# Two-tile residual transfers, a GpSimd-written mask period and an even queue split in an attention and gMLP kernel

## The chip, the cores and the metric

The kernel runs on one NeuronCore of one Trainium2 chip. The metric is device time in microseconds (us) of one execution. Before the change it is 1194.28 us, the median of six executions, which lie between 1193.59 and 1197.21 us. The engines are called by the profile's names: PE (TensorE matmul), PEld (its weight loads), DVE (VectorE), ACT (ScalarE), POOL (GpSimd) and SP (SyncE). Each engine works through its own instructions in order. SP does no arithmetic; it issues DMA transfers. POOL and ACT can issue them too. An issue occupies the issuing engine's queue for some time, and the data lands later.

## The reference

The input is `x` of 2048 tokens by 576 features in bf16. Four layers follow each other, A, B, A, B, each added to `x` after a layer norm. Both A layers share their weights, and so do both B layers.

```python
# A: 32 heads of 18 features; a token sees itself and 7 earlier tokens, 2 apart
idx = pos[:, None] - (arange(8) * 2)[None, :];  mask = idx >= 0
logits = einsum('bhsd,bhswd->bhsw', q, kg) * 18 ** -0.5     # kg, vg: k, v gathered at idx
o = einsum('bhsw,bhswd->bhsd', softmax(where(mask, logits, -1e9)), vg);  return o @ wo
# B: gated MLP that mixes the tokens
z = gelu(x @ w_in);  z1 = z[..., :2304];  z2 = layernorm(z[..., 2304:])
return (z1 * (einsum('ts,bsf->btf', w_sp, z2) + b_sp)) @ w_out

x = x + A(layernorm(x));  x = x + B(layernorm(x))           # twice
```

## The kernel before

Between layers the residual stream lies in DRAM, in the input for the first layer and in `xres[li]` (f32) after it. What the next layer multiplies is held on chip: `xnT` is the normalised `x` with features on partitions and tokens along the free axis. It is filled in tiles of 128 tokens, for most tiles by a DMA transpose on SP (`ln_T`, L249).

**Layer A** (`layer_A`, L322) has two parts. Its instructions are issued in the order in which the code is written.

*Preparation.* `VW` (L373) makes the values of one attention tile. `PG` (L384) multiplies one 128-feature block `d` of queries or keys (`qk`) for one block of 512 tokens (`cc`) and leaves it in a staging tile `stg`, or, for `d` of 3 and 4 in the first token half of the first layer, in the space of the later weight tile `win2a`. When a staging tile is full, its pieces of heads are moved by DMA to `QK`, where a head has a group of 32 partitions to itself; these are the *head moves* (L421). A half of the tokens (`cc` 0 and 1, or 2 and 3) takes 40 of them. They are dealt out in turn to the queues given by name: with `(nc.gpsimd, nc.sync)` each gets every second one, and with `q2 = (nc.gpsimd, nc.sync, nc.gpsimd)` SP gets every third.

Rows 18 to 31 of each 32-partition group hold a bit pattern that makes the dot product of query and key itself put the window's mask in (`build_window_rows`, L115). The first 16 partitions' rows are written to DRAM as `win_period` (L174), loaded into `pat` (`load_pat`, L176) and copied into `QK` by DVE (`fill_window_rows`, L188).

In the first layer (`li == 0`) there is a prologue ahead: `x` is loaded, `S_` takes bn_stats on DVE, `E_` adds epsilon on DVE, `R_` raises to the power -1/2 on POOL, and `A_` normalises on DVE. Tiles 0 to 3 go through PE transposes and an ACT copy into `xnT` (`T_pe`, L561), all others through DMA transposes on SP (`T_`, L569). Those of tiles 12 to 15 stand on SP behind all head moves of the first token half (L631).

*The loop* (L698). Attention works on 19 tiles `t` of 112 queries with 16 earlier keys, each in two halves of the heads, which makes 38 steps `s = 2t + half`. A step runs the scores of the next step (`L_mm`, L426), the exponential on ACT (`EXP`, L440), the values product (`PV`, L447) and then whatever the table has for this step. After every odd step `PV` sends the tile's output through a DMA transpose on SP into `oT` (L467), a ring of 7 tiles of 128 tokens.

The table spreads the rest over the steps (L661 to L683). The remaining `PG` of the second token half stand at steps 0 to 12; the first of them, block 0 of `cc` 3, reads `xnT` of tiles 12 to 15. For output tile `i` of 128 tokens, whose last attention tile is `t`, the step is `s = 2t + 6` in the first layer for `t < 8`, then `2t + 5`, and less at the end:

```python
at(s - 5, XO, i)        # load the residual rows, SP
at(s, WO, i, 0); at(s + 1, WO, i, 1)     # PE: times wo; DVE adds the residual rows into x_new
at(s + 1, LN_STATS, i); at(s + 2, LN_XN, i)
at(s + 2, XST, i)       # store x_new, SP
if i < NS - 1: at(s + 4, LN_T, i)        # transpose for the next layer, SP
```

`XO`'s tile has three buffers and `x_new` four, each of one output tile. So SP carries, for every output tile, a load, a store and two transposes, and in steps 0 to 12 half of the head moves as well.

The program gives the transfers of SP and ACT eight completion counters in turn, and POOL's another eight; a transfer that takes a counter again waits until the transfer that had it last has landed.

**Layer B** (`layer_B`, L714) is three long runs of matmuls: `z` (L782), the token mixing with the gate (`z1` L860 and `gate` L878), and the output (L932), which loads the residual rows and stores the new ones one tile a transfer. The change leaves it alone.

Of the kernel before, what the change touches and what calls it, by code (L numbers as in the profile page):

```python
# [10 lines left out]
ALU = mybir.AluOpType  # L11
AX = mybir.AxisListType
f32 = mybir.dt.float32
bf16 = mybir.dt.bfloat16
# [4 lines left out]
P = 128  # L19
D = 576  # L20
# [7 lines left out]
EPS = 1e-5  # L28
MR = 32 - DH
# [33 lines left out]
class K:  # L63
# [48 lines left out]
        self.xn_rr = 0  # L112
        self.deferred = []

    def build_window_rows(self, c):  # L115

        nc = self.nc
        R = c.tile([P, 2, MR, 16], bf16, name="win_rows")
        self.pat = self.consts.tile([P, 2, 272], bf16, name="win_pat")
        self.patpad = self.consts.tile([P, PADL], bf16, name="win_patpad")
        n = c.tile([P, 3], i32, name="win_n")
        g = c.tile([P, 3], i32, name="win_g")
        bits = c.tile([P, 5, 3], i32, name="win_bits")
        vf = c.tile([P, 5, 3], f32, name="win_vf")
        uu = c.tile([P, 4, 2], f32, name="win_uu")  # L130
        half = WB / 2
        nc.gpsimd.iota(n[:], pattern=[[1, 3]], base=15, channel_multiplier=1)
        nc.gpsimd.memset(R[:, 0, 0:8, :], half)
        nc.gpsimd.affine_select(out=R[:, 0, 0:8, :], in_=R[:, 0, 0:8, :], compare_op=ALU.is_ge, fill=-half,
                                base=1, pattern=[[2, 8], [-1, 16]], channel_multiplier=0)
# [24 lines left out]
        def pads():  # L160
            nc.gpsimd.memset(self.pat[:], 0.0)
            nc.gpsimd.memset(self.patpad[:], 0.0)
            for j in range(4):
                nc.gpsimd.affine_select(out=self.patpad[:], in_=self.patpad[:], compare_op=ALU.not_equal, fill=1.0,
                                        base=-32 * j - 31, pattern=[[0, PADL]], channel_multiplier=1)

        def part1(eng):
            nc.vector.tensor_scalar(out=vf[:], in0=bits[:], scalar1=-2.0, scalar2=1.0, op0=ALU.mult, op1=ALU.add)
            nc.vector.tensor_scalar_mul(out=R[:, :, 0:8, :], in0=R[:, :, 0:8, :], scalar1=vf[:, 4, 1:2])
            nc.vector.tensor_tensor(out=uu[:], in0=vf[:, 0:4, 0:2], in1=vf[:, 0:4, 1:3], op=ALU.add)  # L170
            nc.vector.tensor_scalar_mul(out=R[:, 0, 8:12, :], in0=vf[:, 0:4, 1:2].to_broadcast([P, 4, 16]), scalar1=half)
            nc.vector.tensor_scalar_mul(out=R[:, 1, 8:12, 0:2], in0=uu[:, :, 0:1].to_broadcast([P, 4, 2]), scalar1=0.5)
            nc.vector.tensor_scalar_mul(out=R[:, 1, 8:12, 2:16], in0=uu[:, :, 1:2].to_broadcast([P, 4, 14]), scalar1=0.5)
            self.dma(one[:].rearrange("a r (p f) -> p (a r) f", f=16), R[0:16].rearrange("p a r f -> p (a r) f"), eng=eng)  # L174

        def load(eng):  # L176
            for j in range(4):
                self.dma(self.pat[32 * j + DH:32 * j + 32, :, 0:256], one[:].rearrange("a r x -> r a x"), eng=eng)
        self.load_pat = load
        return part0, pads, part1  # L180
# [141 lines left out]
    def layer_A(self, li):  # L322
        nc, tc, cfg = self.nc, self.tc, self.cfg
        S, NT, XW, NS = cfg.S, cfg.NT, cfg.XW, cfg.NS
# [15 lines left out]
        oT = main.tile([P, 5, RING * P], bf16, name="oT")  # L340
        sb_cm = tc.tile_pool(name=f"A{li}_sb", bufs=2, reuse_waits="tile")
        sb = sb_cm.__enter__()
        if self.right is None:
            self.open_right()
        R = self.right
# [129 lines left out]

        tails = {}

        def XO(i):
            tails[i] = dict(xo=sb.tile([P, D], x_prev_dt, name="xo", tag="xo", bufs=3))
            self.dma(tails[i]["xo"][:], x_prev[i * P:(i + 1) * P, :], eng=nc.sync)  # L480

        def WO(i, hh):
            st = tails[i]
            if hh == 0:
                st["x"] = sb.tile([P, D], f32, name="x_new", tag="x_new", bufs=4)
            r0 = (i % RING) * P
            pw = self.PT_tile([P, 512], f32, "pw")
            for c in range(5):
                nc.tensor.matmul(pw[:, 0:288], lhsT=oT[:, c, r0:r0 + P], rhs=wo_sb[:, c, hh * 288:(hh + 1) * 288],  # L489
                                 start=(c == 0), stop=(c == 4))  # L490
            hs = slice(hh * 288, (hh + 1) * 288)
            nc.vector.tensor_tensor(out=st["x"][:, hs], in0=pw[:, 0:288], in1=st["xo"][:, hs], op=ALU.add)

        def XST(i):
            self.dma(self.xres[li][i * P:(i + 1) * P, :], tails[i]["x"][:])

        def LN_STATS(i):
            tails[i]["ln"] = self.ln_stats(sb, tails[i]["x"], P, want_nmr=False)
# [11 lines left out]
        if li == 0:  # L510
# [19 lines left out]
            warm = self.PT_tile([P, 512], f32, "warm")  # L530
            for _ in range(46):
                nc.tensor.matmul(warm[:, 0:P], lhsT=self.ident[:], rhs=self.ident[:], start=True, stop=True)
            rows = self.build_window_rows(sb)
            nc.scalar.copy(out=v_ext[:, :, :, DH:DH + 1], in_=self.ones[:, None, None, :].to_broadcast([P, NT, H, 1]))
            rows[0]()
            mvs = sb.tile([P, NS, 2], f32, name="lnx_mv", tag="lnx_mv", bufs=1)
# [6 lines left out]
                        nc.vector.bn_stats(out=st[:, s, :], in_=xts[i][:, s * 288:(s + 1) * 288])  # L543
                    nc.vector.bn_aggr(out=mvs[:, i, :], in_=st[:])

            def E_(i0, n):
                nc.vector.tensor_scalar_add(out=rstds[:, i0:i0 + n], in0=mvs[:, i0:i0 + n, 1], scalar1=EPS)

            def R_(i0, n):
                nc.gpsimd.tensor_tensor(out=rstds[:, i0:i0 + n], in0=rstds[:, i0:i0 + n],  # L550
                                        in1=self.neg_half[:, 0:1].to_broadcast([P, n]), op=ALU.pow)
            xns = {}

            def A_(*tiles):
# [15 lines left out]
                for i in tiles:  # L570
                    self.ln_T(xns.pop(i), i * P, P)
            S_(0)
            E_(0, 1)
            R_(0, 1)
            S_(1)
            E_(1, 1)
            R_(1, 1)
            A_(0)
            T_pe(0)
            VW(0, 0, False)  # L580
            VW(0, 1, False)
            S_(2)
            A_(1)
            T_pe(1)
            VW(1, 0, False)
            S_(3)
            E_(2, 2)
            R_(2, 2)
            rows[1]()
            setup_bufs(nc.gpsimd)  # L590
            rows[2](nc.scalar)
            A_(2, 3)
            T_pe(2)
            T_pe(3)
            VW(1, 1, False)
            x_load(sb.tile([P, 4, D], bf16, name="x_in3", tag="x_in", bufs=2)[:], 12, 4, nc.sync)
            S_(4, 5)
            E_(4, 2)
            R_(4, 2)
            VW(2, 0, False)  # L600
            VW(2, 1, False)
# [1 line left out]
            A_(4, 5)  # L603
            T_(4, 5)
            S_(7)
            E_(6, 2)
            R_(6, 2)
            S_(8)
            A_(6, 7)
            T_(6, 7)  # L610
            self.load_pat(nc.sync)
            S_(9, 10, 11)
            E_(8, 4)
            R_(8, 4)
            S_(12)
            A_(8, 9, 10, 11)
            T_(8, 9, 10, 11)
            self.fill_window_rows(QK, 0)
            S_(13, 14, 15)
            E_(12, 4)  # L620
            order = [(d, 0) for d in range(4)] + [(d, 1) for d in range(4)] + [(4, 0), (4, 1)]
            for k_, (d, cc) in enumerate(order):
                for qk in ((1, 0) if d < 4 else (0,)):
                    PG(d, qk, cc, False, (nc.gpsimd, nc.sync) if d in (0, 4) else q2)
                if k_ == 3:
                    VW(3, 0, False)
                    VW(3, 1, False)
                if k_ == 5:
                    R_(12, 4)
                    A_(12, 13, 14, 15)  # L630
# [42 lines left out]
                at(2 * t - 2 + hh, VW, t, hh, 2 * t - 2 + hh >= PG_END and hh == 0)  # L673
        for i in range(NS):
            t = -(-(i + 1) * P // QT) - 1
            s = 2 * t + (6 if li == 0 and t < 8 else 5 if t < NT - 5 else 4 if t < NT - 3 else 3)
            at(s - 5, XO, i)
            at(s, WO, i, 0)
            at(s + 1, WO, i, 1)
# [364 lines left out]
```

The softmax here doesn't subtract the row's maximum and nothing guards it: scores larger than these inputs give would overflow.

## Time and profile before

| | |
|---|---|
| median of six executions | 1194.28 us |
| the profiled execution's own time | 1194.59 us |
| its span from first to last instruction | 1192.8 us |
| PE busy | 1179.4 us (99%) |
| DVE / ACT / POOL busy | 545.5 / 378.5 / 276.9 us |
| mean granted clock of PE | 0.999 |
| first layer, up to the first matmul of B | 0 to 136 us |
| its loop, from the first `PV` on | 48.6 to 136 us |
| first B layer | 136 to 602 us |
| third layer (A) | 602 to 723 us |
| last layer (B) | 723 to 1193 us |
| xo transfers on SP in the A and B layers | 16 of 144 KB, 48 of 288 KB |
| xres stores on SP | 48 of 288 KB |

The profile is of one execution. Its span is 1.8 us shorter than that execution's own time. PE hardly ever rests, so what moves the time is either work added to or taken from PE, a stretch in which PE has to wait, or a stretch in which the clock granted to PE is below 1. [...]

In the timeline, a row is: start in us, length in us, engine, line, operation, output<-input, number of instructions, and in brackets the idle time before it and what ended it. A `q` behind an engine's name (SPq) marks its queue's own work, such as issuing a transfer.

### The profile page before, as it was taken

The numbers are of one execution on the slowest core, as the hardware profiler recorded it, in microseconds if no ns is written. First come the engines' busy times: TensorE is split into PE (matmuls) and PEld (weight loads), VectorE is DVE, ScalarE is ACT, GpSimd is POOL, SyncE is SP. The second block draws the span as 40 slices with busy tenths as digits, with TensorE's granted clock in tenths as the row PEclk, the third lists the DMA queues.
The fourth block names the chain that finished last, engine by engine and source line by source line (L and its number), as shares of the span: only waits on it lengthen the run. The fifth ranks groups of instructions, "written<-read, shape, count | busy, mean of one in ns | idle before, by whom it ended". The sixth has DMA issues, their size and how long they took to land.

```text
span 1192.8 us, 20790 instructions
## 1 busy us (share of the span) xinstructions
PE 1179.4 (99%) x8554; PEld 619.8 (52%) x8554; DVE 545.5 (46%) x1202; ACT 378.5 (32%) x597; POOL 276.9 (23%) x382
## 2 busy tenths in 40 slices
PE   8999999999999999999999999999999999999998
PEld 5566544444444444457755775444444444444676
DVE  9677676333233233245556776763233233232321
ACT  5578677210110110202156786760110110111000
POOL 4668774000000000001153877530000000000000
PEclk9999999999999999999999999999999999999999
DMA  8789791000000000049656799900000000001332
GB/s 197 152 192 230 173 241 38 23 3 10 12 12 12 12 2 10 15 140 286 168 102 119 175 242 190 215 13 10 12 12 1 12 12 12 12 1 33 119 105 73
DMA packets 178791, 101.21 MB, mean 85 GB/s; under 512 B 135039, under 2 KB 160047, under 8 KB 178696
## 3 DMA queue, kind: packets, MB, share of 16 engines
q1 hardware_dynamic: 165400, 78.14, 29.5%
q0 software_dynamic: 6480, 15.99, 5.2%
q10 hardware_dynamic: 6816, 5.77, 1.6%
q8 instruction: 67, 1.10, 0.4%
q14 instruction: 28, 0.23, 0.1%
HBM read 42.39 MB, written 16.53 MB: 49 GB/s over the span
## 4 chain that ended last, share of the span: by engine, by line
PE 94%; DMA 1%; ACT 0%; issue 0%; DVE 0%; SPq 0%; DVEq 0%; ACTq 0%
PE pg L878 42%; PE pz L860 12%; PE po L932 12%; PE pz L782 11%; PE pp L400 4%; PE pw L489 3%; PE O_ps L455 3%; PE pv L377 3%; PE L_ps L435 2%; PE pzs L782 1%; DMA oT<-o_t 1%; ACT P_sb L444 0%; DMA QK<-win2a 0%; PE pt L473 0%; SPq L77 0%
## 5 line engine op out<-in xcount | busy, mean ns | idle before, releaser
L878 PE MATMUL pg<-Wq,Z 128*128 128x512 bf16 x2304 | 502.8, 379 | 0.0
L878 PEld LDWEIGHTS <-Z 128*128 128x128 bf16 x2304 | 225.3, 98 | 272.0
L882 DVE TENSOR_TENSOR g_tmp<-pg,ln_xn 128x512 f32<-128x512 f32 x144 | 99.6, 692 | 428.0 <-PE pg L878 428.0
L872 ACT ACTIVATE z1T<-pz 128x1024 bf16<-128x1024 f32 x72 | 73.7, 1024 | 513.8 <-PE pz L860 513.6
L77 POOL DMA_DIRECT2D wout<-in_B_w_out_dram x4 | 4.2, 1062 | 604.6 <-PE pg L878 604.6
L932 PE MATMUL po<-wout,Z 128*128 128x288 bf16 x1152 | 141.4, 286 | 0.0
L444 ACT ACTIVATE P_sb<-L_ps 128x896 bf16<-128x896 f32 (+1 forms) x152 | 126.7, 887 | 41.8 <-PE L_ps L435 41.1
L860 PE MATMUL pz<-xnT,w 128*128 128x512 bf16 (+1 forms) x640 | 136.0, 380 | 0.0
L932 PEld LDWEIGHTS <-Z 128*128 128x128 bf16 x1152 | 112.7, 98 | 28.8
L782 PEld LDWEIGHTS <-xnT 128*128 128x128 bf16 (+1 forms) x800 | 66.3, 97 | 80.9 <-issue 23.7
L782 PE MATMUL pz<-win2a,xnT 128*128 128x512 bf16 x384 | 104.8, 380 | 0.0
L883 DVE TENSOR_TENSOR Z<-g_tmp,z1T 128x512 bf16<-128x512 f32 x144 | 99.7, 692 | 10.8 <-DVE g_tmp L882 1.4
L860 PEld LDWEIGHTS <-w 128*128 128x128 bf16 (+1 forms) x640 | 51.0, 97 | 80.1 <-issue 27.1
L400 PE MATMUL pp<-xnT,wqk_sb 128*128 128x512 bf16 x360 | 83.5, 382 | 0.0
L796 ACT ACTIVATE zp<-pz 128x1024 bf16<-128x1024 f32 x64 | 65.5, 1024 | 36.7 <-PE pz L782 34.1
L242 POOL TENSOR_SCALAR ln_xn<-x_new,ln_mv,ln_rstd 128x576 bf16<-128x576 f32 x32 | 73.4, 2294 | 2.7
L942 DVE TENSOR_TENSOR x_new<-po,xo 128x288 f32<-128x288 f32 (+1 forms) x64 | 28.8, 456 | 87.9 <-PE po L932 83.9
L782 PE MATMUL pz<-win2b,xnT 128*128 128x512 bf16 (+1 forms) x256 | 65.8, 380 | 0.0
L798 DVE CUSTOM_DVE_ANT_0 Z<-zp 128x1536 bf16<-128x1536 bf16 x32 | 56.4, 1761 | 15.6 <-ACT zp L796 15.5
L77 POOL DMA_DIRECT2D QK<-stg x81 | 50.2, 624 | 38.6 <-DVE stg L369 13.9
L377 PE MATMUL pv<-wv_sb,xnT 128*128 128x288 bf16 (+1 forms) x380 | 56.2, 285 | 2.4 <-ACT xnT L567 2.4
L400 PEld LDWEIGHTS <-wqk_sb 128*128 128x128 bf16 x360 | 33.3, 98 | 36.5 <-issue 0.8
(111 smaller groups left out, 889.9 us busy)
## 6 DMA issues: line engine op xcount, KB each, us to landing
xres<-x_new SPq DMA_DIRECT2D x48, 288.0 KB
xo<-xres SPq DMA_DIRECT2D x48, 288.0 KB
wout<-in_B_w_out_dram POOLq DMA_DIRECT2D x4, 1296.0 KB, 8.0
w<-in_B_w_in_dram SPq DMA_DIRECT2D x16, 256.0 KB
QK<-stg POOLq DMA_DIRECT2D x53, 72.0 KB, 3.8
QK<-stg SPq DMA_DIRECT2D x41, 72.0 KB
xo<-in_A_x_dram SPq DMA_DIRECT2D x16, 144.0 KB
win2a<-in_B_w_in_dram POOLq DMA_DIRECT2D x6, 288.0 KB, 4.7
```

The lines of the kernel that those rows point to most:

```text
L242: e.tensor_scalar(out=xn[:nrows, 0:D], in0=x_t[:nrows, :], scalar1=mv[:nrows, 0:1], scalar2=rstd[:nrows, 0:1], op0=ALU.subtract, op1=ALU.mult)
L377: nc.tensor.matmul(pv[:nk, 0:288], lhsT=self.xnT[:, c, QT * t:QT * t + nk], rhs=wv_sb[:, c, hh * 288:(hh + 1) * 288], start=(c == 0), stop ...
L400: nc.tensor.matmul(pp[:, :], lhsT=w, rhs=self.xnT[:, c, PADL + cc * 512:PADL + (cc + 1) * 512], start=(c == 0), stop=(c == 4))
L444: nc.scalar.activation(out=P_bufs[(2 * s + jp) % 4][:nk, :, :, 0:nq], in_=Lv[:nk, :, :, 0:nq], func=ACT.Exp, scale=scale)
L782: nc.tensor.matmul(pzvs[ci][:, sub * 512:sub * 512 + w], lhsT=self.xnT[r0:r1, c, PADL + i * P:PADL + (i + 1) * P], rhs=win2(c)[r0:r1, c0 + ...
L796: nc.scalar.activation(out=zp[:, c0:c0 + cn], in_=pzvs[ci][:, 0:cn], func=ACT.Gelu_apprx_tanh, accum_out=sums[:, ci:ci + 1])
L860: nc.tensor.matmul(pz1s[q // 2][:, q % 2, :], lhsT=w1[r0:r1, c, sub * P:(sub + 1) * P], rhs=self.xnT[r0:r1, c, PADL + q * 512:PADL + (q + ...
L872: nc.scalar.activation(out=z1T[:, q2 * 512:(q2 + 2) * 512], in_=pz1s[q2 // 2][:, :, :].rearrange("p a b -> p (a b)"), func=ACT.Gelu_apprx_ ...
L878: nc.tensor.matmul(pg[:, :], lhsT=Z[:, jj, i, sub * P:(sub + 1) * P], rhs=Wq[q][:, i, :], start=(i == 0), stop=(i == NS - 1))
L882: nc.vector.tensor_tensor(out=tmp[:], in0=pg[:, :], in1=bsp[:, qs], op=ALU.add)
L883: nc.vector.tensor_tensor(out=uT(jj)[:, sub, qs], in0=tmp[:], in1=z1Ts[jj, sub][:, qs], op=ALU.mult)
L932: nc.tensor.matmul(acc[hh], lhsT=uT(j // 2)[:, j % 2, i * P:(i + 1) * P], rhs=wouts[j // NJH][:, j % NJH, hh * 288:(hh + 1) * 288], start= ...
```

## The change

1. The residual rows of output tiles `i` and `i + 1` are loaded by one transfer, at the even tile's step, and stored by one transfer, at the odd tile's step. The tiles hold two output tiles: two buffers of pairs for `xo` (before: three of one) and two of pairs for `x_new` (before: four of one).
2. `win_period` is written to DRAM from POOL, not from ACT, and the rows it is made from lie in the unused part of `oT`.
3. In the first token half of the first layer all head moves are dealt evenly to POOL and SP.
4. In the prologue, the transpose of tile 1 stands ahead of the first two `VW`, and `E_` is part of `R_`.
5. In the first layer `s = 2t + 6` holds for `t < 10`. Of the output tiles this moves only `i = 7` (`t = 9`), from step 23 to 24.

```diff
@@ layer_A
+        pairs = {k_: sb.tile([P, 2, D], f32, name="x_new", tag="x_new", bufs=2) for k_ in range(2)}
+        xos = {k_: sb.tile([P, 2, D], x_prev_dt, name="xo", tag="xo", bufs=2) for k_ in range(2)}
...
+        def pair_rows(t_):
+            return t_.rearrange("(a p) d -> p a d", p=P)
+
         def XO(i):
-            tails[i] = dict(xo=sb.tile([P, D], x_prev_dt, name="xo", tag="xo", bufs=3))
-            self.dma(tails[i]["xo"][:], x_prev[i * P:(i + 1) * P, :], eng=nc.sync)
+            if i % 2 == 0:
+                xo = xos.pop(i // 2, None) or sb.tile([P, 2, D], x_prev_dt, name="xo", tag="xo", bufs=2)
+                self.dma(xo[:], pair_rows(x_prev[i * P:(i + 2) * P, :]), eng=nc.sync)
+                for k_ in range(2):
+                    tails[i + k_] = dict(xo=xo[:, k_, :])
 
         def WO(i, hh):
+            if i % 2 == 0 and hh == 0 and i > 2:
+                pairs[i // 2] = sb.tile([P, 2, D], f32, name="x_new", tag="x_new", bufs=2)
             st = tails[i]
-            if hh == 0:
-                st["x"] = sb.tile([P, D], f32, name="x_new", tag="x_new", bufs=4)
+            st["x"] = pairs[i // 2][:, i % 2, :]
...
         def XST(i):
-            self.dma(self.xres[li][i * P:(i + 1) * P, :], tails[i]["x"][:])
+            if i % 2 == 1:
+                self.dma(pair_rows(self.xres[li][(i - 1) * P:(i + 1) * P, :]), pairs.pop(i // 2)[:])
...
             T_pe(0)
-            VW(0, 0, False)
-            VW(0, 1, False)
             S_(2)
             A_(1)
             T_pe(1)
+            VW(0, 0, False)
+            VW(0, 1, False)
             VW(1, 0, False)
...
             setup_bufs(nc.gpsimd)
-            rows[2](nc.scalar)
+            rows[2](nc.gpsimd)
...
                 for qk in ((1, 0) if d < 4 else (0,)):
-                    PG(d, qk, cc, False, (nc.gpsimd, nc.sync) if d in (0, 4) else q2)
+                    PG(d, qk, cc, False, (nc.gpsimd, nc.sync))
...
-            s = 2 * t + (6 if li == 0 and t < 8 else 5 if t < NT - 5 else 4 if t < NT - 3 else 3)
+            s = 2 * t + (6 if li == 0 and t < 10 else 5 if t < NT - 5 else 4 if t < NT - 3 else 3)
```

More of the change, by code (lines that the diff above doesn't have):

```diff
@@ L113, in setup, with build_window_rows @@
         self.deferred = []
-    def build_window_rows(self, c):
+    def build_window_rows(self, c, R):
         nc = self.nc
-        R = c.tile([P, 2, MR, 16], bf16, name="win_rows")
         self.pat = self.consts.tile([P, 2, 272], bf16, name="win_pat")
@@ L532, in layer_A @@
                 nc.tensor.matmul(warm[:, 0:P], lhsT=self.ident[:], rhs=self.ident[:], start=True, stop=True)
-            rows = self.build_window_rows(sb)
+            nR = 2 * MR * 16
+            rows = self.build_window_rows(
+                sb, oT[:].rearrange("p a b -> p (a b)")[:, 4 * D:4 * D + nR].rearrange("p (a r f) -> p a r f", a=2, r=MR))
             nc.scalar.copy(out=v_ext[:, :, :, DH:DH + 1], in_=self.ones[:, None, None, :].to_broadcast([P, NT, H, 1]))
@@ L544, in S_ @@
                     nc.vector.bn_aggr(out=mvs[:, i, :], in_=st[:])
-            def E_(i0, n):
-                nc.vector.tensor_scalar_add(out=rstds[:, i0:i0 + n], in0=mvs[:, i0:i0 + n, 1], scalar1=EPS)
             def R_(i0, n):
-                nc.gpsimd.tensor_tensor(out=rstds[:, i0:i0 + n], in0=rstds[:, i0:i0 + n],
-                                        in1=self.neg_half[:, 0:1].to_broadcast([P, n]), op=ALU.pow)
+                rs = rstds[:, i0:i0 + n]
+                nc.vector.tensor_scalar_add(out=rs, in0=mvs[:, i0:i0 + n, 1], scalar1=EPS)
+                nc.gpsimd.tensor_tensor(out=rs, in0=rs, in1=self.neg_half[:, 0:1].to_broadcast([P, n]), op=ALU.pow)
             xns = {}
@@ L572, in layer_A @@
             S_(0)
-            E_(0, 1)
             R_(0, 1)
             S_(1)
-            E_(1, 1)
             R_(1, 1)
@@ L584, in layer_A @@
             T_pe(1)
+            VW(0, 0, False)
+            VW(0, 1, False)
             VW(1, 0, False)
             S_(3)
-            E_(2, 2)
             R_(2, 2)
@@ L597, in layer_A @@
             S_(4, 5)
-            E_(4, 2)
             R_(4, 2)
@@ L605, in layer_A @@
             S_(7)
-            E_(6, 2)
             R_(6, 2)
@@ L612, in layer_A @@
             S_(9, 10, 11)
-            E_(8, 4)
             R_(8, 4)
@@ L619, in layer_A @@
             S_(13, 14, 15)
-            E_(12, 4)
             order = [(d, 0) for d in range(4)] + [(d, 1) for d in range(4)] + [(4, 0), (4, 1)]
```

## The prediction

> **What bounds the kernel now.** The page's first part comes first: PE is busy for 99% of the span, so a microsecond is won or lost only where PE waits or where its granted clock falls. The list of waits then names PE's few waits in the A layers, and the timeline gives their places. The 46.7 to 49 us stretch, where the loop of the first layer begins:
>
> ```profile
> PE 1179.4 (99%) x8554; PEld 619.8 (52%) x8554; DVE 545.5 (46%) x1202; ACT 378.5 (32%) x597; POOL 276.9 (23%) x382
> ...
> 47.45 0.22 PE L435 MATMUL L_ps<-QK 32*128 32x112 bf16 x1 [0.38 <-DMA QK<-win2a]
> 48.44 0.22 PE L435 MATMUL L_ps<-QK 32*128 32x112 bf16 x1 [0.78 <-DMA QK<-win2a]
> 49.02 1.24 PE L400 MATMUL pp<-xnT,wqk_sb 128*128 128x512 bf16 x5
> ```
>
> PE waits 0.38 + 0.78 = 1.16 us for the last head moves, and at 49.02 runs, without a wait, the first PG that reads tiles 12 to 15 of xnT. What the two queues do just before:
>
> ```profile
> 27.78 7.72 SPq L77 DMA_DIRECT2D QK<-stg  x9
> 35.60 5.60 SPq L77 DMA_DIRECT2D QK<-win2a  x7
> 41.30 5.21 SPq L249 DMA_TRANSPOSE xnT<-ln_xn  x4
> 46.56 1.17 SPq L77 DMA_DIRECT2D wo_sb<-in_A_wo_dram  x2
> ...
> 27.25 5.83 POOL L77 DMA_DIRECT2D QK<-stg  x9 [5.24 <-ACT stg L371]
> 34.10 3.62 POOL L77 DMA_DIRECT2D QK<-stg  x6
> 37.72 7.78 POOL L77 DMA_DIRECT2D QK<-win2a  x9
> ```
>
> SP has 16 head moves, POOL 24. SP never rests from 27.78 to 47.7: the 16 moves take 41.30 - 27.78 = 13.5 us, 0.84 each, and the four transposes of tiles 12 to 15 follow at 1.31 each. By the trace's completion events they land at 45.88, 46.79, 47.60 and 48.75. The last is only 0.27 us ahead of the PG at 49.02.
>
> The other places are in the loops, where PE waits for oT, and one stretch at half clock:
>
> ```profile
> 102.47 0.79 PE L489 MATMUL pw<-wo_sb,oT 128*128 128x288 bf16 x5 [0.99 <-DMA oT<-o_t]
> 107.17 0.79 PE L489 MATMUL pw<-wo_sb,oT 128*128 128x288 bf16 x5 [0.25 <-DMA oT<-o_t]
> ...
> 694.54 0.79 PE L489 MATMUL pw<-wo_sb,oT 128*128 128x288 bf16 x5 [0.84 <-DMA oT<-o_t]
> ...
> 59.79:63.20 3.41, 2.73 (x62) 1.00 0.54 134
> 63.20:66.61 3.41, 3.41 (x50) 0.50 0.98 199
> ```
>
> The last two rows are windows (stretch, length, PE busy and instructions, granted clock, DMA share, GB/s).
>
> **The change part by part**, against the profiled execution's 1194.59 us (span 1192.8 and 1.8 around it; 0.31 above the median).
>
> *Even shares of the head moves.* SP gets 20, POOL 20. SP cannot begin before 27.78, because its transposes of tiles 8 to 11 fill it until 27.67 and DVE's chain sets those. 20 moves at the measured pitches (blocks 0 to 3: 3.58 + 3 x 3.37, block 4: 3.18 us) end at 44.7. The four transposes then are issued from 44.7 to 49.9, the last at 48.7. From issue to landing, the last one took 3.47 us before, with POOL's late moves still in flight, and 2.63 at 26.44 with little beside it. POOL is now done by about 41, so the second row is nearer: landing at 51.3 (ends: 51.3 and 52.2). The PG that ran at 49.02 now starts then. **Cost +2.3 us**, ends +2.2 and +3.1. The PG stands in PE's order ahead of all of the loop, and what follows is driven by PE, so nothing absorbs it. That the last head move lands earlier on POOL's side is worth nothing: PE would reach the PG sooner and wait there.
>
> *win_period from POOL.* ACT loses one issue (0.34 us); POOL gets it behind its memsets, at 12.3, ahead of the R_ at 12.78. POOL's issues in the trace take 0.5 to 1.2 us, so this R_ slips 0.3 to 0.9 and A_ of tiles 4 and 5 with it. DVE's later wait of 0.59 us for the oT load (at 16.08) takes that up, except perhaps 0.4 that would push SP's start. I take +0.2 (0 to +0.45). The load of pat comes at 20.35, well after.
>
> *Prologue order.* Before, the three stalls in front of VW cost PE 0.79 + 0.81 + 0.79 us. With the second transpose at 7.7, when its input is ready (A_ ends at 7.65), ACT's copies run beside VW and PG starts near 12.9, not 14.15; its weights have landed for the first block at 12.03. This 1.3 us lies ahead of the SP-bound landing: **0**. If that cover were gone it would be worth up to -1.3. E_ keeps its place on DVE: 0.
>
> *Clock.* Between the last pre-loop PG (about 46) and 51.3, PE now has only one L_mm and one PV to do. The row of 59.79 to 63.20 shows that a stretch with one PG, three L_mm and two PV, with just 0.68 us of stalls in it, already halved the clock for the next 3.41 us; the PG in there took 2.29 us, not 1.24, and the L_mm 0.58, not 0.40: 1.2 us lost. The 46.13 to 49.55 window with 1.16 us of stalls and about 1 us of PG did not. The new stretch is poorer in work than either. I take **+1.0 us**, ends 0 (the windows cut it luckily) and +2.4 (two windows).
> The Trainium skill ("TensorE: Matmul & The Clock Gate", Part 1) says the clock halves after a whole idle window of some 3.4 us and that the windows run freely. By it, no single stall here is long enough, this term is 0 and the sum falls to 1196.5. The row above, busy 2.73 of 3.41 us and halved all the same, speaks against reading "idle" so strictly.
>
> *Pairs of residual rows, layer 1.* SP is saved every second xo (0.45 us) and xres (0.57 us). It was late with oT by 4 us at 101.65. By step 21 some five such issues count after its last rest at 72 to 73.9 us, 2.5 us, so the oT transposes come earlier even with 288 KB more in one store ahead of them (1.4 us at 210 GB/s). With tile 7 one step later, both stalls go: -1.24. But step 23 now has no WO, and PE meets ACT there as it does in step 22 (0.33 us for P_sb at 99.98): +0.4. **Net -0.85**, ends -1.24 and 0.
>
> *Pairs, layer 3.* Here xo is f32. SP would issue the transpose that PE awaits at 694.54 only 0.85 us earlier (o_t is ready at about 687.6, the issue was at 688.51), and a store and a load of two tiles stand right ahead of it, 288 KB more than before in all. The DMA share is 1.66 in 688 to 692. I take **0**, ends -0.84 and +1.0.
>
> *Buffers.* x_new's pair is free again only when the later tile's store has landed: 3 to 4 steps (6.4 to 8.5 us) lie between that store and the next use, where a single tile had 6. In the first layer tiles 4 and 5 need the store of 0 and 1, issued about 83.8 in the old clock, landing 87.7 (2.5 us by the row of 84.39, and 1.4 for its size); DVE wants it at 87.1. In the third, tiles 6 and 7 need a store that lands near 682.4, wanted at 681.7. Queued behind such a wait on DVE are the reciprocal and o_t of the next PV, and PE waits once the four PT buffers are full, 1.3 steps later. DVE is busy 3.3 of 4 us there and recovers slowly. I take **+0.3**, ends 0 and +2.
>
> Sum: 2.3 + 0.2 + 0 + 1.0 - 0.85 + 0 + 0.3 = +2.95, so **1197.5 us**, 0.27% above the median.
>
> **Rivals.**
> - *Nearly nothing.* The clock holds and both loops lose all their oT stalls: 2.5 - 1.24 - 0.84 = +0.4, 1195.0 us. For it: only one window in the first loop was halved. Against: step 23 runs into ACT.
> - *Faster.* SP's 0.83 us a move is partly contention with POOL, and the pitch falls to about 0.6, so the last transpose lands by 48. This is where it decides: the 1.16 us stall goes, and with -0.85 and -0.84 in the loops it is 1194.6 - 2.85 = 1191.7, or 1191.2 with what is left of the prologue's gain. Against: SP's pitch is 0.78 + 0.05 at 54 us too, when hardly anything else is under way.
> - *The stores bite.* DVE's waits for x_new reach PE in several of the six reuses in each loop: about 0.5 us each for six of them is 3 more, 1200.5. For it: margins of 0 us in two places that I could work out; against: late DVE work has a step of slack.
>
> **How the numbers follow.** Forecast 0.57, nothing 0.22, faster 0.11, stores 0.10. A measurement here can tell about 0.2%, 2.4 us: faster is below 1191.9, slower above 1196.7. The forecast's own range is 1196.0 to 1199.0, of which 0.07 lies within the band; so slower 0.50 + 0.10 = 0.60, same 0.22 + 0.07 = 0.29, faster 0.11. The range 1192.5 to 1201 leaves out most of the faster case and the far end of the stores and the clock.
>
> **What would show it.** Right: SP issues 20 head moves in a row from about 27.8 to 44.7, its four transposes end near 50, and the first PG behind the first PV starts at 51 to 52 after a wait of some 2 to 3 us for xnT; a halved window starts between 49 and 53; the pw waits at steps 23 and 25 are gone and a P_sb wait stands in step 23. Wrong: the PG at 49 us not waiting, or a pitch of SP's moves well off 0.83; DVE waiting for xres; a new pw wait of more than 1 us in the third layer.

## The result and the profile after

The changed kernel takes 1197.55 us, the median of 19 runs (1196.03 to 1202.39); beside it the kernel before takes 1195.18 us, the median of 39 runs (1192.6 to 1199.0). The ratio of the two is 1.0022, with a 95% interval of 1.0013 to 1.0031: slower by 2.6 us by the ratio and by 2.4 us between the medians, about 0.2%. Single executions of either kernel lie more than 6 us apart. The prediction said 1197.5. In both, the profiled execution is not quite the median: the one of the changed kernel took 1200.06 us, 2.5 above its median, the one before 1194.59 us.

From the page of the changed kernel, the engines' busy time, and behind it three rows of the list of waits (engine, tile and line, what it waits for, us in total, times, longest):

```profile
PE 1182.4 (99%) x8554; PEld 621.6 (52%) x8554; DVE 545.4 (46%) x1202; ACT 378.2 (32%) x597; POOL 276.1 (23%) x379
...
PE pp L401 <- DMA xnT<-ln_xn: 4.2, 1, 4.2
PE pw L497 <- DMA oT<-o_t: 2.9, 2, 1.7
...
DVE x_new L500 <- DMA xres<-x_new: 0.2, 1, 0.2
```

The first wait is new. Its place in the timeline of the changed kernel, where the loop of the first layer begins, and the queues ahead of it:

```profile
46.61 0.56 PE L456 MATMUL O_ps<-v_ext,P_sb 128*128 128x19 bf16 x16
51.34 2.29 PE L401 MATMUL pp<-xnT,wqk_sb 128*128 128x512 bf16 x5 [4.17 <-DMA xnT<-ln_xn]
...
27.59 10.32 SPq L77 DMA_DIRECT2D QK<-stg  x12
38.01 6.45 SPq L77 DMA_DIRECT2D QK<-win2a  x8
44.57 5.21 SPq L248 DMA_TRANSPOSE xnT<-ln_xn  x4
49.83 1.18 SPq L77 DMA_DIRECT2D wo_sb<-in_A_wo_dram  x2
...
38.81 4.94 POOL L77 DMA_DIRECT2D QK<-win2a  x4 [0.41 <-issue]
```

SP issues 20 head moves from 27.59 to 44.47 and the four transposes until 49.78. By the completion events of the trace they land at 47.20, 49.16, 49.87 and 51.20 us, and PE starts 0.14 us after the last. POOL has been done since 43.8. Before, the same PG ran at 49.02 without a wait.

The clock, in windows of the changed kernel (start and end, length, busy time and instructions of PE, PEld, DVE, ACT, POOL, granted clock, DMA share, GB/s):

```profile
47.10:50.50 3.40, 0.07 (x3) 0.00 (x0) 0.72 (x2) 1.56 (x2) 0.00 (x0) 1.00 0.74 142
50.50:53.90 3.40, 2.56 (x21) 0.92 (x21) 0.18 (x1) 0.00 (x0) 0.00 (x0) 0.50 0.72 200
53.90:57.30 3.40, 3.40 (x50) 1.40 (x39) 1.61 (x4) 1.73 (x2) 0.00 (x0) 0.50 0.17 35
```

PE is all but idle from 47.1 to 50.5, and the next two windows run at half clock; the halved window that the kernel before has from 63.2 to 66.6 is gone. The waits for `oT` have changed places too (timeline of the changed kernel, first and third layer):

```profile
95.47 0.79 PE L497 MATMUL pw<-wo_sb,oT 128*128 128x288 bf16 x5 [1.18 <-DMA oT<-o_t]
...
698.80 1.23 PE L497 MATMUL pw<-wo_sb,oT 128*128 128x288 bf16 x5 [1.72 <-DMA oT<-o_t]
```

The two profiled executions differ by 5.5 us of span, and the starts of PE's stages say where: the PG behind the first PV 2.32 us later; from there to the first matmul of B (at 131.64 us before, where the attention's last matmuls still run until 135.9) 83.68 us against 82.62 (+1.06); from the first PV of the third layer to B 87.78 against 85.52 (+2.27). The two B layers are as long as before (470.19 and 470.35 us). The last of the three is more than belongs to the median, as the experiments show.

### The profile page after: what moved, and what is told of

Read it like the earlier page. It is cut to its first block, busy times and chain, and to the rows that moved or that the text cites. A ratio compares the mean times of both kernels' runs of the same rounds, so it can differ in the third digit from the quotient of the medians.

```text
span 1198.3 us, 20731 instructions
## 1 busy us (share of the span) xinstructions
PE 1182.4 (99%) x8554; PEld 621.6 (52%) x8554; DVE 545.4 (46%) x1202; ACT 378.2 (32%) x597; POOL 276.1 (23%) x379
## 4 chain that ended last, share of the span: by engine, by line
PE 95%; DMA 2%; DVE 1%; ACT 1%; SPq 1%; issue 1%; POOL 0%; POOLq 0%
PE pg L880 41%; PE pz L862 12%; PE po L934 12%; PE pz L784 11%; PE pp L401 6%; PE pw L497 3%; PE pv L378 3%; PE O_ps L456 3%; PE L_ps L436 2%; PE pzs L784 1%; DMA oT<-o_t 1%; SPq L77 1%; ACT P_sb L445 0%; DMA QK<-stg 0%; DVE ln_st L554 0%
## 5 line engine op out<-in xcount | busy, mean ns | idle before, releaser
L401 PE MATMUL pp<-xnT,wqk_sb 128*128 128x512 bf16 x360 | 84.5, 385 | 4.2 <-DMA xnT<-ln_xn 4.2
```

Source lines behind the costliest of these rows:

```text
L401: nc.tensor.matmul(pp[:, :], lhsT=w, rhs=self.xnT[:, c, PADL + cc * 512:PADL + (cc + 1) * 512], start=(c == 0), stop=(c == 4))
```

## Experiments

Each run stands beside executions of the kernel before on the same chip; a ratio is to these, with its 95% interval. The experiments were run in three groups, each with its own executions of the kernel before, so its median differs a little between them (1195.38, 1196.42 and 1196.04 us).

### The queue shares alone, both ways

The changed kernel with the old queues:

```diff
-                    PG(d, qk, cc, False, (nc.gpsimd, nc.sync))
+                    PG(d, qk, cc, False, (nc.gpsimd, nc.sync) if d in (0, 4) else q2)
```

> The kernel after with the head moves dealt out as before (SP 16, POOL 24). Queue theory: SP's four transposes of tiles 12 to 15 are issued from about 41.2 us and land by 48.8, the first PG behind the first PV starts at 48.5 to 49 instead of 51.3, the granted clock is not halved between 50 and 57 us, and the time falls by 2.3 us for the wait and about 1.5 for the clock, to 1193.5 to 1194.5. Pairs theory (the paired loads and stores are what costs): the PG comes earlier, but the time stays at 1197 or more, since what is lost is lost in the loops of layers 1 and 3.

The kernel before with the even shares is the same line the other way round.

> The kernel before with only the even shares (SP 20, POOL 20). Queue theory: the PG at 49.0 moves to 51.3 to 52 behind a wait of 3 to 4 us for xnT, the clock is halved for one or two windows after it, and the time rises by 2.3 us and 1 to 2 us for the clock, to 1198 to 1199.5. Pairs theory: at most 1 us more than before, 1195.2 to 1196.

| | median us | before us | ratio | PG behind the first PV | its wait for xnT |
|---|---|---|---|---|---|
| changed, old queues | 1194.55 | 1195.38 | 0.9991 (0.9981 to 1.0001) | 49.55 | 0.40 |
| before, even queues | 1197.57 | 1195.38 | 1.0021 (1.0008 to 1.0033) | 51.01 | 3.25 |

The even shares alone make all of the loss, and without them the loss is gone. Both times are just outside what was expected (1193.5 to 1194.5, and 1198 to 1199.5), and one point failed: the changed kernel with the old queues was to keep its full clock, but its profile has a halved window too, from 49.76 to 53.18 us. In the timeline of the kernel before with even queues, SP's queue and then PE:

```profile
27.18 10.33 SPq L77 DMA_DIRECT2D QK<-stg  x12
37.61 6.56 SPq L77 DMA_DIRECT2D QK<-win2a  x8
44.27 5.20 SPq L249 DMA_TRANSPOSE xnT<-ln_xn  x4
...
51.01 0.59 PE L400 MATMUL pp<-xnT,wqk_sb 128*128 128x512 bf16 x1 [3.25 <-DMA xnT<-ln_xn]
```

It is the same picture as in the changed kernel, 0.3 us earlier: the 20 moves, the four transposes behind them and PE waiting for the last.

### Is it SP's late landing, or something else that goes with the even shares?

The changed kernel, with the even shares kept, but tiles 13 to 15 transposed by PE, so that only one transpose is left behind SP's 20 moves:

```diff
-            T_(12, 13, 14, 15)
+            T_(12)
+            for i in (13, 14, 15):
+                T_pe(i)
```

> The changed kernel, but xnT of tiles 13 to 15 comes from PE transposes and an ACT copy, as tiles 0 to 3 do; only tile 12 is left on SP behind the 20 head moves. PE gets 15 small matmuls more, 1.2 us by the row of the prologue (0.79 us for ten). Theory (the loss is SP's late landing and nothing else): SP's one transpose lands near 47.2, PE comes to the PG behind the first PV at about 47.8 and does not wait for xnT, no halved window before 57; against 51.34 that is 3.5 us less, so 1194.0 us, faster than the changed kernel and, by 1.2 us, than the kernel before. Rival (the late PG costs little, the loss lies in the two loops' waits for oT and their clock): the PG comes early all the same, but the loops lose it again and the time stays at 1197 us.

Measured: 1193.85 us against 1196.04, ratio 0.9983 (0.9970 to 0.9995). This beats both kernels, though by little. Its timeline, SP's queue and PE:

```profile
27.22 10.33 SPq L77 DMA_DIRECT2D QK<-stg  x12
37.66 6.46 SPq L77 DMA_DIRECT2D QK<-win2a  x8
44.22 1.25 SPq L248 DMA_TRANSPOSE xnT<-ln_xn  x1
45.52 1.17 SPq L77 DMA_DIRECT2D wo_sb<-in_A_wo_dram  x2
...
34.20 1.13 PE L574 MATMUL pt<-ident,ln_xn 128*128 128x128 bf16 x15 [0.55 <-DVE ln_xn L567]
...
47.40 0.56 PE L456 MATMUL O_ps<-v_ext,P_sb 128*128 128x19 bf16 x16
47.82 1.24 PE L401 MATMUL pp<-xnT,wqk_sb 128*128 128x512 bf16 x4
```

SP's moves end where they did (44.12), but the PG runs at 47.82 without a wait and at full clock, for 1.13 us of transposes on PE. Expected were 47.8 and 1194.0 us. Each measured against the kernel before beside it, the changed kernel's +2.37 us became -2.19: 4.6 us from taking three transposes out of that place, of which 3.5 are the PG's start. The two halved windows near 50 us are gone as well, but the next experiment gives the clock little of the other 1.1 us, and I cannot assign them. The rival, that the loops lose it again, falls.

The same without the pairs and with tile 7 at its old step (the kernel before with even queues, `win_period` from POOL, the new prologue order and the PE transposes):

> The kernel before with even shares of the head moves, win_period from POOL, the new prologue order and PE transposes of tiles 13 to 15; residual rows one tile a transfer and tile 7 at its old step. It differs from the run above by the pairs and tile 7 only. If pairs move waits about and cost nothing: within 0.5 us of the run above, 1194. If the transfers of 576 KB ahead of oT's transposes cost 0.5 to 1.5 us, which the two other runs with pairs leave open: 1192.5 to 1193.5. If the pairs gain (my step 5, -0.85): 1194.9.

Measured: 1195.16 us, ratio 1.0004 (0.9987 to 1.0022); the PG starts at 47.89, again without a wait. So the version with pairs is 1.3 us the faster here. The two intervals overlap, and the single profiles point the other way (spans 1193.5 with pairs, 1191.8 without). It speaks for a small gain from the pairs and tile 7's later step together and does not prove one.

### Can the wait be filled, or moved?

Filled: 20 matmuls behind the first PV of the changed kernel.

```diff
+            if li == 0 and s == 0:
+                warm2 = self.PT_tile([P, 512], f32, "warm2")
+                for _ in range(20):
+                    nc.tensor.matmul(warm2[:, 0:512], lhsT=self.ident[:], rhs=wqk[:, 0, 0:512], start=True, stop=True)
```

> The kernel after with 20 matmuls of 128 by 512 on data at hand, whose result is not used, right behind the first PV, where PE waits 4.2 us for xnT. They take 4.3 us. Clock theory: the PG starts at 51.3 as before, the clock stays full from 46 to 57 us, and the time falls by 1.5 to 2.5 us, to 1195 to 1196. If the halved clock does not come from that wait, or costs little, the time stays within 0.7 us of 1197.5.

Measured: 1197.25 us, ratio 1.0021 (1.0011 to 1.0031), 0.3 us below the changed kernel. The fill did what it was made for, and the clock was then halved elsewhere (timeline, then windows, of this kernel):

```profile
46.64 4.48 PE L708 MATMUL warm<-wqk_sb,ident 128*128 128x512 bf16 x19
51.51 1.24 PE L401 MATMUL pp<-xnT,wqk_sb 128*128 128x512 bf16 x5 [0.40 <-DMA xnT<-ln_xn]
```

```profile
62.90:66.30 3.40, 2.67 (x67) 2.01 (x68) 1.66 (x4) 3.21 (x5) 1.96 (x4) 1.00 0.66 137
66.30:69.70 3.40, 3.40 (x38) 1.48 (x38) 1.86 (x4) 1.76 (x3) 1.52 (x3) 0.50 1.17 190
```

The PG takes 1.24 us again, not 2.29. But the stretch with two waits for ACT (64.33 and 65.14 us), which in the changed kernel stood at 66.64 and 67.45 and was not followed by a halved window, here is followed by one, as in the kernel before. In this profile the loop is 1.2 us shorter than in the changed kernel's (82.46 against 83.68), and the medians show 0.3. The expectation's second case, a halved clock that costs little, is what came out.

The mean granted clock, which is recorded to three places for every execution, says the same of more than one profile. It is 0.9992 over the 12 executions with the fill, 0.9974 over those of the changed kernel and 0.9979 over the 35 of the kernel before that ran beside the fill. One halved window of 3.41 us lowers such a mean by 0.0014, so these are, as an estimate, 0.6, 1.8 and 1.5 halved windows an execution. The fill thus gave the changed kernel a better clock than the kernel before has, and the time stayed 1.0021 of the latter's: the loss does not rest on the clock. What the fill itself may cost I did not separate, so a small share stays possible.

Moved: the loop's PG of the first layer two steps later, with two steps of attention ahead of them.

```diff
-            at((k_ * PG_END) // len(pgs), PG, d, qk, cc, True)
+            at(2 + (k_ * 12) // len(pgs) if li == 0 else (k_ * PG_END) // len(pgs), PG, d, qk, cc, True)
```

> The changed kernel, but in the first layer the PG of the loop stand at steps 2 to 13, not 0 to 13, so that two steps of attention come ahead of the PG that reads tiles 12 to 15. My first step said that nothing absorbs that PG's wait because of its place in PE's order. If that is so, the wait for xnT goes: L_mm and PV of two steps (some 1.9 us of PE) run before 51.3, and the time falls by 1 to 1.9 us to 1195.6 to 1196.5. If PE only waits elsewhere in that stretch (for ACT's exponentials, 1.7 us each, and at half clock) or in the denser steps behind it: 1197 to 1198.

Measured: 1202.55 us, ratio 1.0059 (1.0041 to 1.0076). Neither number was met; it is 5 us worse than the changed kernel. The timeline of this kernel, PE and, last, DVE:

```profile
48.31 0.37 PE L436 MATMUL L_ps<-QK 32*128 32x112 bf16 x8 [0.72 <-ACT P_sb L445]
...
53.19 0.58 PE L401 MATMUL pp<-xnT,wqk_sb 128*128 128x512 bf16 x1 [1.58 <-DMA xnT<-ln_xn]
...
94.47 0.27 PE L436 MATMUL L_ps<-QK 32*128 32x112 bf16 x1 [3.45 <-DMA QK<-stg]
95.62 0.46 PE L436 MATMUL L_ps<-QK 32*128 32x112 bf16 x7 [0.88 <-DMA QK<-stg]
97.41 0.65 PE L436 MATMUL L_ps<-QK 32*128 32x112 bf16 x2 [1.32 <-DMA QK<-stg]
...
93.53 0.46 DVE L500 TENSOR_TENSOR x_new<-pw,xo 128x288 f32<-128x288 f32 x1 [4.34 <-DMA xres<-x_new]
```

PE did use the time before 51, though with waits for ACT, and the wait for `xnT` shrank to 1.58 us, although SP's last transpose landed later than in the changed kernel, at 53.05 for 51.20. What I had not seen is that these PG have a date on the other side. Their last eight head moves are issued from 84.5 us on, for 82.7 in the changed kernel; by the completion events they take 8.6 to 10 us to land, where those took 3.7 to 5.2, and the scores of step 18 wait 5.65 us for them. In the same crowd a paired store, issued at 83.39, lands at 93.34, and DVE stands 4.34 us for its buffer. That the moves land so late because the two PG steps less leave them closer together is my reading; no run separates it.

### The pairs

In the kernel before: loads and stores in pairs; loads alone; stores alone. The edits are those of `XO`, `WO` and `XST` in the diff.

> The kernel before with only the pairs of residual rows. Queue theory: the PG at 49.0 stays. The waits for oT at steps 23 and 25 of the first loop shrink or go, a new one of about 1 us at step 18 comes (behind the paired store), and the third layer's wait grows from 0.8 to about 1.7 us; in all 0 to 1.5 us more than before, 1195 to 1196.7. Pairs theory: the whole of the change's loss, 1197.5.

> The kernel before with only the residual rows' loads in pairs; the stores stay one tile each. If the paired stores are what delays oT, this one gains a little: the waits of 1.24 us at steps 23 and 25 of the first loop go, the third layer's stays at 0.8, none comes at step 18: 0 to 1.2 us less than before. If the loads do it (a load of 576 KB stands right ahead of the transpose in the third layer), the third layer's wait is 1.5 us or more.

> The kernel before with only the stores in pairs. If the paired stores delay oT: waits for oT of 1 us and more in both loops, as with both in pairs, 0.5 to 1.7 us more than before. If not: no more waiting than before.

| | median us | before us | ratio | oT waits over 0.5 us in the profile |
|---|---|---|---|---|
| both | 1197.06 | 1195.38 | 1.0013 (0.9998 to 1.0027) | 0.51, 0.96; layer 3: 0.61 |
| loads | 1196.62 | 1196.42 | 0.9996 (0.9979 to 1.0013) | 0.70, 0.62; layer 3: 0.60, 0.56 |
| stores | 1195.89 | 1196.42 | 1.0002 (0.9985 to 1.0018) | 0.99, 0.88; layer 3: 1.43 |

(Three of these waits, 0.51, 0.62 and 0.99, the profile puts down to PE itself; in each the `oT` transpose landed 0.09 us before the matmul, so they are counted here.) None differs from the kernel before by more than can be told, and in none do the waits for `oT` vanish. They move to other steps. The first of the three came out nearer to the pairs theory's 1197.5 than to the 1195 to 1196.7 of the other; what speaks against that theory is the changed kernel with the old queues, which has the pairs and is not slower. The loads alone are within what was expected of them (0 to 1.2 us less), and the stores alone brought the waits that were expected but not the 0.5 to 1.7 us. Why the waits do not vanish is seen in the chain of waits of the changed kernel:

```profile
88.46 6.97 DMA oT<-o_t
...
690.34 8.41 DMA oT<-o_t
```

The transpose that PE awaits at 95.47 was issued at 88.46, straight behind the first paired store (87.25) and took 6.97 us to land; the one awaited at 698.80 was issued at 690.34 behind a paired store (689.14) and a paired load (689.77) and took 8.41, where the one of 694.54 before took 5.98. SP issues less, and what it issues last lands later. Over the profiles this holds as a mean: an `oT` transpose takes 4.7 us to land in the first layer's loop and 4.9 in the third's in the six kernels with paired stores (the moved PG left out), 4.3 and 4.4 in the six without pairs. A single long one proves nothing: 8.65 us occurs without pairs as well.

Over all profiles of this study, the stretch from the first PV of the third layer to B is 85.3 to 87.8 us, mean 86.2, in the seven kernels with paired stores, and 84.5 to 86.0, mean 85.1, in the six without pairs. In the first layer's loop, from the PG behind the first PV on, it is 82.0 to 83.7, mean 82.9, in the six with paired stores (the moved PG left out), and 82.6 to 86.6, mean 84.3, in the six without. The kernel with paired loads alone, in neither group, has 86.0 and 84.1. With one profile for each kernel this is a hint, not a proof: a gain in the first layer that the third takes back.

In the profiles with paired loads in the kernel before (both and loads alone) the first B layer is also 1.7 us longer, 0.9 of it a wait of `pz` for ACT. The changed kernel, which has paired loads too, does not show it. I did not find why.

### Prologue, win_period and tile 7

The kernel before with the new prologue order and `win_period` from POOL:

```diff
+            S_(2)
+            A_(1)
+            T_pe(1)
             VW(0, 0, False)
             VW(0, 1, False)
-            S_(2)
-            A_(1)
-            T_pe(1)
...
-            rows[2](nc.scalar)
+            rows[2](nc.gpsimd)
```

> The kernel before with the new prologue order and win_period from POOL; queues, pairs and tile 7 as before. My steps 2 and 3 say: the first PG starts near 12.9 instead of 14.2, SP's head moves start at 27.6 to 28.2 all the same, the PG behind the first PV at 48.7 to 49.5, and the time is that of the kernel before within 0.5 us, 1195.4. Rival: the 1.3 us of the prologue are kept, 1194.1. Rival: POOL's issue delays SP's start by 0.4 us, 1195.8.

Measured: 1196.41 us against 1196.04, ratio 1.0004 (0.9991 to 1.0017). PE has the gain and gives it back (timeline of this kernel):

```profile
12.89 1.24 PE L400 MATMUL pp<-xnT,wqk_sb 128*128 128x512 bf16 x4
...
47.10 0.20 PE L435 MATMUL L_ps<-QK 32*128 32x112 bf16 x1 [0.82 <-DMA QK<-win2a]
48.14 0.42 PE L435 MATMUL L_ps<-QK 32*128 32x112 bf16 x8 [0.83 <-DMA QK<-win2a]
48.90 0.22 PE L435 MATMUL L_ps<-QK 32*128 32x112 bf16 x1 [0.34 <-DMA QK<-win2a]
49.05 0.56 PE L455 MATMUL O_ps<-v_ext,P_sb 128*128 128x19 bf16 x16
49.60 1.63 PE L400 MATMUL pp<-xnT,wqk_sb 128*128 128x512 bf16 x4
```

The first PG starts at 12.89, not 14.15, and the waits for the last head moves grow from 1.16 to 1.99 us; the PG behind the first PV comes at 49.60.

The new prologue order with tile 7's later step, and `win_period` still from ACT:

> The kernel before with only the new prologue order and the later step of output tile 7. The PG behind the first PV stays at 48.7 to 49.1 although PE begins its first PG 1.3 us earlier (the prologue's gain is covered by SP); the waits for oT at steps 23 and 25 (1.24 us) go and one of 0.3 to 0.4 for P_sb comes: 0.5 to 0.9 us less than before. If the prologue's gain is not covered, 1.8 us less.

Measured: 1197.21 us against 1196.42, ratio 1.0005 (0.9991 to 1.0019). The prologue's gain did not appear (first PG at 14.23): `VW` of tile 1 waited 1.37 us for an ACT copy into `xnT`. ACT's copies began at 12.25 there, behind the issue of `win_period` at 11.88, and at 10.92 in the changed kernel. In the seven profiles with `win_period` on POOL the first PG starts at 12.47 to 12.91, in the seven with it on ACT at 13.46 to 14.55, the two with the new order among the latest (14.23 and 14.41). So the order alone is not worth anything; whether moving `win_period` alone would do, no run shows. Tile 7's step did not rid the loop of its waits for `oT` either, 1.76 us at 113.70.

A third queue: on top of this, block 4's head moves shared between ACT and POOL and block 2's dealt evenly, SP left with 14 in all.

```diff
+                    PG(d, qk, cc, False, (nc.gpsimd, nc.sync) if d in (0, 2) else q2 if d < 4 else (nc.scalar, nc.gpsimd, nc.scalar))
```

> As the previous kernel (one tile a transfer, new prologue order, later step of tile 7), and the first token half's head moves dealt to three queues: SP 14, POOL 21, and ACT 5 of block 4, where ACT has 4.7 us to itself. Queue theory: SP's transposes end near 45 and land by 47.7, the PG behind the first PV starts at 47.5 to 48, and the time falls by 1.2 us for that and 0.8 for the loop against before: 1193 to 1193.5. If what counts is not SP's queue but the transfers' own speed, the PG does not move from 49.

Measured: 1199.31 us against 1196.42, ratio 1.0020 (1.0003 to 1.0037): a miss. SP's queue and PE in this kernel's timeline:

```profile
28.14 14.87 SPq L77 DMA_DIRECT2D QK<-stg  x11
43.11 2.42 SPq L77 DMA_DIRECT2D QK<-win2a  x3
45.64 5.20 SPq L249 DMA_TRANSPOSE xnT<-ln_xn  x4
...
35.88 5.01 ACTq L77 DMA_DIRECT2D QK<-win2a  x5
...
52.41 0.58 PE L400 MATMUL pp<-xnT,wqk_sb 128*128 128x512 bf16 x1 [3.61 <-DMA xnT<-ln_xn]
```

SP had 14 moves and finished them at 45.53, later than 20 in the changed kernel: two pauses of 2.7 and 2.8 us stand between them, while ACT's five transfers are under way. SP's transfers share eight completion counters with ACT's, and the list of waits of SP's queue in this kernel names earlier head moves as what ended the pauses:

```profile
SPq L77 <- DMA QK<-win2a: 2.8, 1, 2.8
SPq L77 <- DMA QK<-stg: 2.7, 1, 2.7
```

By the completion events, the move of 37.85 was issued 0.06 us after the transfer that had its counter last had landed (one of SP's own, at 37.79), and the move of 41.42 0.01 us after ACT's first one had (41.41; it took 5.5 us). So ACT's moves took counters that SP then lacked: a third queue with the same counters is not a free one. The run also shows the mechanism of the even shares once more: the last transpose landed at 52.28, and PE began at 52.41.

## Why the prediction was right, step by step

The sum came out at 1197.5 against 1197.55 measured, and the wait that carries it was foreseen in its place and in the time at which it ends. That the two numbers agree to 0.05 us is luck: the sum added 2.95 us to one execution of 1194.59, while beside its own executions of the kernel before (1195.18) the changed kernel is 2.4 us slower, and the terms other than the first were off in both directions.

- **Even shares, +2.3: right.** Said: 20 moves to 44.7, transposes issued until 49.9, the last landing at 51.3. Seen: 44.47, 49.78, 51.20, and the last latency 2.65 us for the 2.63 taken. The runs with the shares alone, both ways, and with the transposes taken off SP show this as the cause. PE's wait was 4.17 us, not 2 to 3, because PE came to it earlier (first PV at 46.61 for 48.59), which costs nothing, as the step itself says. One thing flatters the number: the 49.02 us of the profile before was an early one. In the seven kernels of this study with the old shares the PG began at 48.7 to 51.2, mean 49.7, and in the three with the even shares and nothing else altered there (changed, filled, and before with even queues) at 51.0 to 51.5, mean 51.3. Over several executions the shift is thus nearer 1.6 than 2.3.
- **win_period from POOL, +0.2: nothing.** The issue took 0.84 us and ended right ahead of R_, which ran at 13.00 instead of 12.78; SP's moves began at 27.59, not after 27.78. (POOL's issues before take up to 1.48 us, not the 1.2 that was read.)
- **Prologue, 0: right**, and for the reason given, SP's late landing; with the old shares the gain is spent on the head moves. PG began at 12.91 for the 12.9 said.
- **Clock, +1.0: the halved windows came, the cost is not borne out.** Two halved windows began at 50.5, the upper end given (two windows), and the older one at 63.2 vanished, for which the term took nothing off. By the mean clocks the changed kernel has only some 0.3 halved windows more an execution than the kernel before (an estimate from 0.9974 and 0.9979), four of the seven kernels with the old shares have one near 50 us too, and filling the wait was worth 0.3 us in the median. The Trainium skill ("TensorE: Matmul & The Clock Gate", Part 1) gives half clock to a whole idle window of some 3.4 us; the window ahead of the first of them, 0.07 us busy, is as good as idle and agrees, but the second followed a window with 2.56 us of work.
- **Pairs in the first layer, -0.85: mis-sized.** Both waits named, at steps 23 and 25, are gone, as said; the P_sb wait feared for step 23 did not come (the one of 0.27 us at 104.80 stands in step 22, as 0.33 did before). But a new wait of 1.18 us at 95.47, in step 18, was not foreseen. I had let 1.4 us for the 288 KB more ahead of an `oT` transpose be outweighed by SP's earlier issue; the transpose took 6.97 us. In its profile the net is about -0.1.
- **Pairs in the third layer, 0: the profile shows +0.88** in that wait (1.72 for 0.84) and the halved window that followed; this is within the ends given with it, but a new `pw` wait of over 1 us there was also named as a sign of being wrong. It belongs to this execution, which lies 2.5 us above the median: the changed kernel with the old queues has 0.63 us there, with the filled wait 0.77 and 0.26, with the PE transposes none.
- **x_new buffers, +0.3: 0 in this profile (0.2 us of DVE's time).** The mechanism exists. DVE's waits for the paired store add up to 1.5 to 2.7 us in five other profiles with paired stores, and to 8.2 us where the PG were moved. No wait of PE names it, not even with the moved PG, where PE waits for head moves.
- **Taken together** the parts other than the shares change the time by about -1 us (the changed kernel with old queues, 0.9991), of which the interval leaves -2.3 to +0.1; the forecast's terms for them sum to -0.35.

The rivals: "nearly nothing" had the clock hold and all waits for `oT` go; neither happened. "Faster" needed a pitch of SP's moves of 0.6 us; it was 0.84 (16.9 us for 20). The row cited against it, at 54 us, was weaker than said, as POOL issues four moves in that stretch too (from 53.62). "The stores bite" was not what cost the time here; with the moved PG it shows on DVE (4.34 us), beside PE's own wait for head moves.

## What to carry to other kernels

Where two queues share work, count what else stands behind it on each: an even split of the moves was uneven in the end, because SP had 5.2 us of transposes to issue behind its share, and PE's next instruction needed the last of them. Merging transfers saves issues, but a transfer that the compute engine awaits then lands behind more bytes (here 0.4 to 0.5 us later on average); and before work is put off to fill a wait, look for its own date at the other end.

## What the runs showed of the chip that I had not expected

- **How the clock follows the load.** I cut the two A layers of all profiles of this study, from 40 us on, into the windows of 3.41 us that the clock's changes mark. All 16 windows in which PE was busy for less than 1.9 us were followed by one at half clock, and of those with more than 2.9 us none was. In between it goes both ways: ten were, at least thirty were not. Two windows of the kernel before and then one of the changed kernel with old queues, each with the window after it:

```profile
46.13:49.55 3.42, 2.27 (x38) 1.21 (x37) 0.32 (x2) 2.48 (x4) 0.00 (x0) 1.00 0.87 206
49.55:52.96 3.41, 3.41 (x66) 1.78 (x64) 2.49 (x5) 2.18 (x4) 0.00 (x0) 1.00 0.22 73
59.79:63.20 3.41, 2.73 (x62) 1.76 (x60) 1.76 (x4) 3.21 (x5) 1.55 (x4) 1.00 0.54 134
63.20:66.61 3.41, 3.41 (x50) 1.58 (x47) 1.41 (x3) 1.37 (x3) 2.13 (x4) 0.50 0.98 199
```

```profile
90.72:94.13 3.41, 1.95 (x38) 1.16 (x34) 2.25 (x8) 1.39 (x3) 3.07 (x3) 1.00 1.31 184
94.13:97.54 3.41, 3.41 (x65) 2.68 (x62) 2.38 (x9) 3.37 (x5) 3.21 (x5) 1.00 1.08 358
```

  2.27 and 1.95 us busy were let pass, 2.73 was not. Busy time alone does not decide it, then; where the idle time lies in the window, and how much of PE's array the matmuls used, I did not separate.
- **Halved windows of neighbouring poor stretches are not added up.** Eight of the 14 profiles have a halved window that begins between 49 and 52 us, and none of these has another before 90; of the six without it, four have one that begins between 62 and 67 (the kernel before and the filled wait among them). So a new halved window can stand in the place of an old one. Why, I did not separate.
- **The landing of the last head moves and transposes of the first token half varies by 1 to 2 us between profiles with the same queues.** Over the seven kernels with the old shares SP's last transpose took 3.4 to 4.9 us (3.47 in the profile before, 4.27 in the changed kernel with the old queues), and the longest head move took 5.7 to 6.7. In one group of runs, 35 executions of the kernel before spread over 1191.8 to 1199.7 us, more than any one step here is worth.
